# A hand-made order for the first rows, and gaps between the operand places

## The chip, the cores and the metric

The kernel runs on one core of a Trainium2 chip. The metric is the device time of one execution in microseconds; the time before is the median of three runs, 887.15 us (886.62 to 887.22). A profile of one execution shows what each engine did: TensorE (PE, with its weight loads as PEld), VectorE (DVE), ScalarE (ACT), GpSimd (POOL), and SyncE (SP), which here only starts DMAs.

## The reference

From x (2048 tokens by 640 channels, float32) the reference makes the layer-normalized xn, and returns the sum of x, a Fourier mixing of xn and a token MLP on a second normalization of xn:

```
xn = layernorm(x)
a  = xn @ hid_re.T ;  b = xn @ hid_im.T          # 640 x 640 matrices
A  = seq_re @ a - seq_im @ b                     # 2048 x 2048 matrices
h  = layernorm(xn)
u  = gelu(h.T @ w1 + b1)                         # 640 x 1728, over the tokens
B  = (u @ w2 + b2).T
return x + A + B
```

## The kernel before

All products are float32 by three products of halves: an operand is split in a part rounded to the matrix format ("high", made by ACT, line 111) and the rest ("low", made by DVE, line 114), and `three` (lines 119 to 124) issues high by high, high by low and low by high into one PSUM bank. The sums that a fast matrix multiplication (seven products in place of eight) needs are made by DVE between the stages.

The work runs in one list of steps. A step takes one raw piece of a matrix, 128 rows by up to 640 columns, cuts it into high and low in one of three places `cut0` to `cut2`, and issues its products. The piece for step i + 2 is cut while step i multiplies (AHEAD = 2), and raw pieces are loaded some steps earlier by DMAs from SP's queue.

The stages, in order:

- First columns (16 steps, 80 groups of three products): the first eight row blocks of x (128 tokens each), normalized, times the first 512 columns of both 2048-wide matrices. The steps go through the two matrices m = 0 and 1 one after the other, and in each through the eight row blocks k. Each step multiplies by all five 128-channel parts of the row block.
- Seven more column stages of 32 steps, first with the upper half of the rows of x (the operand places `n00` to `n03`), then with the lower half (`n10` to `n13`).
- The hidden matrices, then the MLP up and down. In these the piece is the stationary operand, and the moving one, 320 columns wide, is read from the places that are then called `shid`, `sup` and `sdown`.

In the first columns and the column stages the stationary operand (128 columns) is read from the places `n`, and the moving one (512 columns) from `cut0` to `cut2`. A place `n` is a slab of 17,920 bytes per partition (tags `slab0` to `slab7`: `n00` to `n03` are slab0 to slab3, `n10` to `n13` are slab4 to slab7). The slabs, the pieces (16,384 bytes) and the cuts (5,120 bytes) are all multiples of 256 bytes, so the offset to 256 bytes changes only where small tiles lie between them. Tiles lie in the order in which they are first asked for. `slab7` is asked for first (as `idle`, line 104), at byte 16,672 of the partition: offset 32. Then come three tiles of 128 bytes (`mv`, `norm`, `again`), and then all other places, at offset 160.

| place | offset before | offset after |
| --- | --- | --- |
| n00, n01, n02, n03 | 160, 160, 160, 160 | 0, 64, 96, 128 |
| n10, n11, n12, n13 | 160, 160, 160, 32 | 160, 192, 96, 224 |
| cut0, cut1, cut2 | 160, 160, 160 | 224, 32, 96 |
| raw pieces, results | 160 | 160 |

At the start the rows must be normalized before the first product. The chain for one row block is: DMA of the row block; `moments` (two `bn_stats` and one `bn_aggr` on DVE); `root` (DVE, then a square root on ACT); `inverse` and `offset` (DVE); `normalize` (ACT, in place); `high` (ACT) and `low` (DVE). `first_rows` holds the last three. Twenty products of zeros (WARM, lines 107 and 108) run on TensorE until the data are there. The first eight steps are not recorded under the manual schedule: the scheduling layer orders their instructions on each engine, and from step 8 on they stand as they are written (`by_hand = 8`). ROWS_AT and GROUPS_AT say at which step which rows are loaded and have their factors made.

Of the kernel before, what the change touches and what calls it, by code (L numbers as in the profile page):

```python
# [8 lines left out]
F32 = mybir.dt.float32  # L9
# [5 lines left out]
P = 128  # L15
S = 2048
D = 640
F = 1728
# [10 lines left out]
EPS = 1e-5  # L29
AHEAD = 2  # L30
LOADS = 4
WARM = 20


ROWS_AT = {0: (0,), 1: (1,), 2: (2, 3), 3: (4, 5), 4: (6, 7)}
GROUPS_AT = {0: ((1, 2), (2, 4)), 1: ((4, 6),), 3: ((6, 8),)}

BLOCK = 16
GROUP = 32


# [13 lines left out]
def fnet_plus_mixer(  # L55
# [36 lines left out]

    b1_sb = keep.tile([P, NFB], F32, name="b1_sb")
    b2_sb = keep.tile([P, NS], F32, name="b2_sb")
    out_rows = [out[t * P : (t + 1) * P, :] for t in range(NS)]
    x_rows = [x[t * P : (t + 1) * P, :] for t in range(NS)]
    part_up = [dram.tile([P, 2, D], F32, name=f"up{r}") for r in range(NF2)]
    y_part = [[dram.tile([P, ND, CH], F32, name=f"y{m}{c}") for c in range(NC)] for m in range(2)]


    one = keep.tile([P, 1], F32, name="one")
# [8 lines left out]
    def high(hi, src):  # L110
        nc.scalar.activation(hi, src, AF.Copy)  # L111

    def low(lo, src, hi):
        nc.vector.tensor_sub(lo, src, hi.bitcast(F32))  # L114
# [4 lines left out]
    def three(psum, w, m, first, last):  # L119

        (wh, wl), (mh, ml) = w, m
        nc.tensor.matmul(psum, wh, mh, start=first, stop=False, skip_group_check=True)  # L122
        nc.tensor.matmul(psum, wh, ml, start=False, stop=False, skip_group_check=True)  # L123
        nc.tensor.matmul(psum, wl, mh, start=False, stop=last, skip_group_check=True)  # L124
# [16 lines left out]
    def cut_piece(source, n):  # L141

        held = {}

        def top():
            cut_turn[0] = (cut_turn[0] + 1) % (AHEAD + 1)
            held["piece"] = keep.tile([P, 2, D], R32, name="piece", tag=f"cut{cut_turn[0]}")
            high(held["piece"][:, 0, :n], source())

        def bottom():  # L150
            hi, lo = (held["piece"][:, i, :n] for i in range(2))
            low(lo, source(), hi)
            return hi, lo

        return top, bottom


    mv = keep.tile([P, NS, 2], F32, name="mv")

    norm = keep.tile([P, 2, NS], F32, name="norm")  # L160
    again = keep.tile([P, 2, NS], F32, name="again")
# [29 lines left out]
    def factors(ks):  # L191
        inverse(norm[:, 0, ks], *root(mv[:, ks, 1]))
        offset(norm, ks)
# [15 lines left out]

        return [rooted, inverted]  # L210

    def normalize(k, row, by):
        nc.scalar.activation(row, row, AF.Identity, scale=by[:, 0, k : k + 1], bias=by[:, 1, k : k + 1])  # L213


    def pair_at(tag):
# [27 lines left out]
    def fifth(a, which, i):  # L244
        return a[:, which, 7 * Q + i * P : 7 * Q + (i + 1) * P]

    def place_fixed(h, q):
        fixed[h][q] = keep.tile([P, 2, 8 * Q], R32, name=f"n{h}{q}", tag=f"slab{4 * h + q}")

    def sums_of_rows(h, q, row, lower, apart=False):  # L250
# [37 lines left out]
        return [job1, job2, job3, job4] + [job5] * apart + [job6]  # L288


    x_slab = [
        keep.tile([P, 7, D], F32, name="x0", tag="slab4"), keep.tile([P, 1, D], F32, name="x1", tag="slab5"),
    ]
    x_in = [x_slab[k // 7][:, k % 7, :] for k in range(8)]
# [37 lines left out]
    def later_moments(q):  # L332

        def get():
            for i in range(2):
                nc.sync.dma_start(later_pair(q)[:, i, :], x_rows[8 + q + 4 * i])

        loads[6 + 2 * q].append(get)
        for i in range(2):
            extras[8 + 2 * q + i].append(lambda i=i: moments(8 + q + 4 * i, later_pair(q)[:, i, :]))  # L340

    def later_factors():

# [49 lines left out]
    def c_tile():  # L393

        i = c_turn[0] = (c_turn[0] + 1) % 6
        return c_place[i // 3][:, i % 3, :]

    def store_y(h, m, c, j, t):
        if h == 0:
            nc.gpsimd.dma_start(y_part[m][c][:, j, :], t)  # L400
        else:
            nc.gpsimd.dma_start(y_part[m][c][:, j, :], t, accum_op=ALU.add)

    def first_columns():

        raw = pieces[1].rearrange("p a q c -> p (a q) c")
        banks = {}
        for i in range(BLOCK):
            m, k = i // 8, i % 8

            def load(m=m, k=k, i=i):
                if m == 0:
                    for r in ROWS_AT.get(k, ()):
                        nc.sync.dma_start(x_in[r], x_rows[r])  # L414
                nc.sync.dma_start(raw[:, i % 8, :], dft_seq[m * NC, k])

            def rows(m=m, k=k):
                if m == 0:
                    first_rows(k)
                    for k0, k1 in GROUPS_AT.get(k, ()):  # L420
                        for r in range(k0, k1):
                            moments(r, x_in[r])
                        factors(slice(k0, k1))

            def products(w, m=m, k=k):
                for j in range(ND):
                    if k == 0:
                        banks[j] = psum[(5 * m + j) % 8]
                    three(banks[j], channels(k, j), w, k == 0, k == 7)

            def read(m=m):
                for j in range(ND):
                    c = c_tile()
                    nc.scalar.activation(c, banks[j], AF.Copy)
                    store_y(0, m, 0, j, c)

            loads[i - LOADS].append(load)
            sums[i - AHEAD].append(rows)
            steps.append(cut_piece(lambda i=i: raw[:, i % 8, :], CH) + (products,))
            if k == 7:  # L440
                reads[i + 1].append(read)
        loads[-LOADS].append(lambda: None)

    def columns(g, h, c):

# [363 lines left out]
        )  # L809


    first_columns()
    first_sums = [sums_of_rows(0, q, lambda q=q: x_in[q], lambda q=q: x_in[q + 4], True) for q in range(4)]
    for q in range(4):
        later_moments(q)
    timed[8].append(lambda: jobs.extend(j for part in (slice(4), slice(4, 6)) for js in first_sums for j in js[part]))
    for g in range(2 * NC - 1):
        columns(g, (g + 1) // NC, (g + 1) % NC)
    s_rows = BLOCK
# [37 lines left out]
    for t in range(NS // 2):  # L857
        down(1, t, ("ca", "cb")[t % 2])

    ready = {}  # L860

    def do_jobs(n, short=False):

        while n > 0 and jobs and not (short and isinstance(jobs[0], tuple)):
# [86 lines left out]
```

## Time and profile before

| what | us |
| --- | --- |
| median of three runs | 887.15 |
| the profiled execution | 887.16 |
| its span, first to last instruction | 884.9 |
| PE busy | 877.2 |
| PEld busy | 798.8 |
| DVE busy | 701.8 |
| ACT busy | 525.5 |
| first product of the data (after the products of zeros) | at 9.42 |
| first 320-wide product | at 411.66 |
| last product starts | at 880.78 |

A product's time in the groups (391 ns for 512 columns) is longer than the step from one start to the next, since products overlap in the pipeline. What counts is the step from start to start, which is read from the list of instructions in order of time, or from the number of products in a stretch.

### The profile page before, as it was taken

The page shows a single profiled execution, that of the slowest core. Times are in us where ns is not written, and L with a number is a line of the kernel's source. Part 1 is how long each engine was busy: PE and PEld are TensorE (multiplying, and loading weights), DVE is VectorE, ACT ScalarE, POOL GpSimd, SP SyncE. Part 2 cuts the span into 40 slices and gives each one's busy share as a digit, 9 for nine tenths or more (in the row PEclk, how much of TensorE's full clock was granted, in tenths as well). Part 3 has the DMA queues.
Part 4 walks back from the last instruction along what each step waited for, and adds up shares of the span by engine and source line. Part 5 has one row for each costly group of instructions (what it writes and reads, how often), then busy time and mean ns, then how long its engine had stood idle before and what let it go on. Part 6 is the DMA issues. An engine that isn't in the chain of part 4 may idle for free.

```text
span 884.9 us, 14021 instructions
## 1 busy us (share of the span) xinstructions
PE 877.2 (99%) x4964; PEld 798.8 (90%) x4964; DVE 701.8 (79%) x1181; ACT 525.5 (59%) x953; POOL 123.2 (14%) x166
## 2 busy tenths in 40 slices
PE   8999999999999999999999999999999999999998
PEld 5888888888888888888999999999999999999998
DVE  8577888796787978787877887998678968986776
ACT  6546576664565566557565555675477766655553
POOL 0101000101121111222010101000122211111111
PEclk9999999999999999999999999999999999999999
DMA  8941463719475555869766766553478797756875
GB/s 292 319 144 66 151 253 102 268 48 329 87 206 89 154 136 114 225 83 184 180 124 156 163 142 193 159 180 133 131 170 182 174 253 183 164 129 133 156 173 124
DMA packets 85542, 147.15 MB, mean 166 GB/s; under 512 B 8416, under 2 KB 35296, under 8 KB 85216
## 3 DMA queue, kind: packets, MB, share of 16 engines
q1 hardware_dynamic: 64848, 95.72, 33.3%
q0 software_dynamic: 20624, 50.54, 30.0%
q8 instruction: 39, 0.64, 0.3%
q14 instruction: 31, 0.25, 0.1%
HBM read 99.63 MB, written 51.84 MB: 171 GB/s over the span
## 4 chain that ended last, share of the span: by engine, by line
PE 96%; DVE 2%; ACT 1%; DMA 1%; issue 0%; SPq 0%
PE psum L124 32%; PE psum L123 32%; PE psum L122 32%; DMA pieces<-in_dft_seq 1%; DVE piece L114 0%; DVE st L166 0%; ACT x L213 0%; DVE n L114 0%; DVE shid L114 0%; ACT piece L111 0%; DVE pair L117 0%; DVE pieces L662 0%; DVE pieces L117 0%; SPq L414 0%; ACT shid L111 0%
## 5 line engine op out<-in xcount | busy, mean ns | idle before, releaser
L114 DVE TENSOR_TENSOR piece<-pieces,piece 128x512 fp32r<-128x512 f32 (+2 forms) x506 | 346.6, 688 | 147.7 <-ACT piece L111 144.3
L111 ACT ACTIVATE piece<-pieces 128x512 fp32r<-128x512 f32 (+2 forms) x506 | 317.9, 629 | 235.1 <-PE psum L124 161.0
L122 PE MATMUL psum<-piece,n 128*128 128x512 f32 x584 | 228.4, 391 | 2.5 <-ACT n L111 2.5
L123 PE MATMUL psum<-piece,n 128*128 128x512 f32 x584 | 228.3, 391 | 0.0
L124 PE MATMUL psum<-piece,n 128*128 128x512 f32 x584 | 227.4, 391 | 0.0
L122 PEld LDWEIGHTS psum<-piece,n 128*128 128x128 f32 x584 | 109.6, 188 | 27.2 <-ACT n L111 3.8
L123 PEld LDWEIGHTS psum<-piece,n 128*128 128x128 f32 x584 | 109.7, 188 | 25.6 <-DVE piece L114 2.0
L124 PEld LDWEIGHTS psum<-piece,n 128*128 128x128 f32 x584 | 109.7, 188 | 23.1
L124 PE MATMUL psum<-sup,piece 128*128 128x320 f32 x392 | 121.5, 310 | 0.0
L124 PE MATMUL psum<-sdown,piece 128*128 128x320 f32 x392 | 121.1, 309 | 0.0
L123 PE MATMUL psum<-sdown,piece 128*128 128x320 f32 x392 | 121.0, 309 | 0.0
L123 PE MATMUL psum<-sup,piece 128*128 128x320 f32 x392 | 121.0, 309 | 0.0
L122 PE MATMUL psum<-sup,piece 128*128 128x320 f32 x392 | 121.0, 309 | 0.0
L122 PE MATMUL psum<-sdown,piece 128*128 128x320 f32 x392 | 121.0, 309 | 0.0
L117 DVE TENSOR_TENSOR pieces<-pieces 128x512 f32<-128x512 f32 (+3 forms) x142 | 112.5, 793 | 2.6
L124 PE MATMUL psum<-shid,piece 128*128 128x320 f32 x280 | 86.9, 310 | 0.1
L123 PE MATMUL psum<-shid,piece 128*128 128x320 f32 x280 | 86.5, 309 | 0.0
L122 PE MATMUL psum<-shid,piece 128*128 128x320 f32 x280 | 86.5, 309 | 0.0
L712 ACT ACTIVATE pair<-psum 128x320 f32<-128x320 f32 x104 | 45.3, 436 | 60.1 <-PE psum L124 59.6
L124 PEld LDWEIGHTS psum<-sup,piece 128*128 128x128 f32 x392 | 73.6, 188 | 0.3
L122 PEld LDWEIGHTS psum<-sup,piece 128*128 128x128 f32 x392 | 73.6, 188 | 0.0
L123 PEld LDWEIGHTS psum<-sup,piece 128*128 128x128 f32 x392 | 73.6, 188 | 0.0
(95 smaller groups left out, 1007.8 us busy)
## 6 DMA issues: line engine op xcount, KB each, us to landing
pieces<-in_dft_seq SPq DMA_DIRECT2D x128, 256.0 KB, 5.6
pieces<-in_w SPq DMA_DIRECT2D x88, 256.0 KB, 3.8
y<-c POOLq DMA_DIRECT2D x84, 256.0 KB, 6.0
out<-pair POOLq DMA_DIRECT2D x38, 320.0 KB, 5.2
pieces<-y SPq DMA_DIRECT2D x32, 320.0 KB, 3.7
pieces<-in_w SPq DMA_DIRECT2D x32, 192.0 KB, 3.1
out<-in_x SPq DMA_DIRECT2D x16, 320.0 KB, 5.9
up<-pair POOLq DMA_DIRECT2D x8, 640.0 KB, 3.3
```

Of the source, the lines that this page charges most:

```text
L111: nc.scalar.activation(hi, src, AF.Copy)
L114: nc.vector.tensor_sub(lo, src, hi.bitcast(F32))
L117: nc.vector.tensor_sub(to, a, b)
L122: nc.tensor.matmul(psum, wh, mh, start=first, stop=False, skip_group_check=True)
L123: nc.tensor.matmul(psum, wh, ml, start=False, stop=False, skip_group_check=True)
L124: nc.tensor.matmul(psum, wl, mh, start=False, stop=last, skip_group_check=True)
L712: nc.scalar.activation(c, b, AF.Copy)
```

## The change

The order of the first columns is written out. `FIRST` lists 18 steps as (m, k, first part, last part): row blocks 0 and 1 are multiplied by both matrices at once (all five parts with m = 0, three parts with m = 1), then row blocks 2 to 7 with m = 0, then 2 to 7 with m = 1, and at the end the two parts that were left of blocks 0 and 1 with m = 1. Within a step the products go by kind: high by high for all parts, then high by low, then low by high. `START` is a string of words, one for each operation up to step 7, in the order in which they are recorded, now all under the manual schedule: x and b load, T and B cut, M, R, F make moments, root and factors, H normalizes straight into the high part, N normalizes in place (for later sums), L makes the low part, P multiplies, e loads later rows. Row block 0 comes in two halves, one from ACT's queue ahead of its first work and one from SP's. WARM is 13 in place of 20.

`mv`, `norm` and `again` are asked for ahead of all places, and `pad` puts a tile of 32 or 64 bytes, filled once by POOL, between the places: the offsets are in the table above. The numbers of products, cuts, row operations and stores are the same; there are ten small fills on POOL, one more DMA and one more ACT instruction. The order of the last two jobs of `first_sums` changes, and they start at step 10 in place of 8.

```
-WARM = 20
-ROWS_AT = {0: (0,), 1: (1,), 2: (2, 3), 3: (4, 5), 4: (6, 7)}
-GROUPS_AT = {0: ((1, 2), (2, 4)), 1: ((4, 6),), 3: ((6, 8),)}
-BLOCK = 16
+WARM = 13
+BLOCK = 18
+FIRST = (
+    [(0, 0, 0, 5), (1, 0, 0, 3), (0, 1, 0, 5), (1, 1, 0, 3)] + [(0, k, 0, 5) for k in range(2, 8)]
+    + [(1, k, 0, 5) for k in range(2, 8)] + [(1, 0, 3, 5), (1, 1, 3, 5)]
+)
+START = """
+    x0 b0 x1 b1 b2 x2 b3 x3 b4 x4 x5 b5 x6 x7 b6 b7
+    T0 M0 R0 F0 H0 B0 N0 M1 R1 T1 L0 F1 H1 B1 P0
+    M2 T2 N1 B2 L1 b8 P1 M3 T3 R2-3 F2-3 H2 B3 P2
+    M4 T4 N2 B4 L2 b9 P3 M5 H3 T5 R4-5 N3 B5 F4-5 L3 b10 e0 P4
+    M6 H4 T6 N4 B6 L4 b11 P5 H5 M7 R6-7 T7 N5 B7 F6-7 L5 b12 e1 P6
+    H6 T8 M8 N6 B8 L6 b13 P7 H7 T9 M12 N7 B9 L7
+"""
+    def pad(n):
+        gap = keep.tile([P, n // 4], F32, name=f"gap{gaps[0]}")
+        gaps[0] += 1
+        nc.gpsimd.memset(gap, 0.0)
+    x_slab = [keep.tile([P, 7, D], F32, name="x0", tag="slab4")]
+    pad(32)
+    x_slab.append(keep.tile([P, 1, D], F32, name="x1", tag="slab5"))
+    pad(32)
+    nc.scalar.dma_start(x_in[0][:, H2:], x_rows[0][:, H2:])
...
         def top():
+            if gaps[0] < 10:
+                pad(64)
...
     for q in range(4):
+        pad((32, 64, 32, 32)[q])
         place_fixed(0, q)
+    pad(32)
-    def first_rows(k):
-        normalize(k, x_in[k], norm)
+    def first_rows(k, which):
...
-        high(two(0), src)
-        high(fifth(a, 0, k // 4), x_in[k][:, 2 * Q :])
-        low(two(1), src, two(0))
-        low(fifth(a, 1, k // 4), x_in[k][:, 2 * Q :], fifth(a, 0, k // 4))
+        for to, t in whole:
+            if which == 0:
+                normalize(k, t, norm, to(0))
+            else:
+                low(to(1), t, to(0))
...
+            for n, (rows, cols) in enumerate(((0, 0), (0, 1), (1, 0))):
+                for j in range(j0, j1):
...
+                    nc.tensor.matmul(
+                        banks[m, j], channels(k, j)[rows], w[cols], start=n == 0 and k == begin,
+                        stop=n == 2 and k == end, skip_group_check=True,
+                    )
...
-    by_hand = 8
-    for i in range(-LOADS, by_hand):
-        if i == -AHEAD:
-            moments(0, x_in[0])
-            factors(slice(0, 1))
-        turn_of(i, 0)
     with tc.manual_schedule():
-        for i in range(by_hand, len(steps) + 1):
+        for word in START.split():
+            start[word[0]](*map(int, word[1:].split("-")))
+        for i in range(8, len(steps) + 1):
```

More of the change, by code (lines that the diff above doesn't have):

```diff
@@ L31 @@
 LOADS = 4
-WARM = 20
-ROWS_AT = {0: (0,), 1: (1,), 2: (2, 3), 3: (4, 5), 4: (6, 7)}
-GROUPS_AT = {0: ((1, 2), (2, 4)), 1: ((4, 6),), 3: ((6, 8),)}
-BLOCK = 16
+WARM = 13
[4 more added lines that the diff above has]
+)
+FIRST_AT = [0, 6, 1, 7, 2, 3, 4, 5, 0, 1, 2, 3, 4, 5, 0, 1, 6, 7]
+START = """
[6 more added lines that the diff above has]
+"""
 GROUP = 32
@@ L94, in fnet_plus_mixer @@
     b2_sb = keep.tile([P, NS], F32, name="b2_sb")
+    one = keep.tile([P, 1], F32, name="one")
+    mv = keep.tile([P, NS, 2], F32, name="mv")
+    norm = keep.tile([P, 2, NS], F32, name="norm")
+    again = keep.tile([P, 2, NS], F32, name="again")
+    def pad(n):
+        gap = keep.tile([P, n // 4], F32, name=f"gap{gaps[0]}")
+        gaps[0] += 1
+        nc.gpsimd.memset(gap, 0.0)
+    gaps = [0]
     out_rows = [out[t * P : (t + 1) * P, :] for t in range(NS)]
     x_rows = [x[t * P : (t + 1) * P, :] for t in range(NS)]
+    x_slab = [keep.tile([P, 7, D], F32, name="x0", tag="slab4")]
+    pad(32)
+    x_slab.append(keep.tile([P, 1, D], F32, name="x1", tag="slab5"))
+    pad(32)
+    x_in = [x_slab[k // 7][:, k % 7, :] for k in range(8)]
+    nc.scalar.dma_start(x_in[0][:, H2:], x_rows[0][:, H2:])
     part_up = [dram.tile([P, 2, D], F32, name=f"up{r}") for r in range(NF2)]
     y_part = [[dram.tile([P, ND, CH], F32, name=f"y{m}{c}") for c in range(NC)] for m in range(2)]
-    one = keep.tile([P, 1], F32, name="one")
     nc.vector.memset(one, 1.0)
@@ L155, in cut_piece @@
         return top, bottom
-    mv = keep.tile([P, NS, 2], F32, name="mv")
-    norm = keep.tile([P, 2, NS], F32, name="norm")
-    again = keep.tile([P, 2, NS], F32, name="again")
     def moments(k, row):
@@ L210, in factors_again, with normalize @@
         return [rooted, inverted]
-    def normalize(k, row, by):
-        nc.scalar.activation(row, row, AF.Identity, scale=by[:, 0, k : k + 1], bias=by[:, 1, k : k + 1])
+    def normalize(k, row, by, to=None):
+        nc.scalar.activation(
+            row if to is None else to, row, AF.Identity, scale=by[:, 0, k : k + 1], bias=by[:, 1, k : k + 1]
+        )
     def pair_at(tag):
@@ L288, in sums_of_rows @@
         return [job1, job2, job3, job4] + [job5] * apart + [job6]
[L291 to L294, printed above, removed]
     for q in range(4):
+        pad((32, 64, 32, 32)[q])
         place_fixed(0, q)
-    def first_rows(k):
-        normalize(k, x_in[k], norm)
+    pad(32)
+    def first_rows(k, which):
         a = fixed[0][k % 4]
@@ L307, in two @@
             return part(a, which, 1, 2).rearrange("p (b c) -> p b c", b=2)
-        high(two(0), src)
-        high(fifth(a, 0, k // 4), x_in[k][:, 2 * Q :])
-        low(two(1), src, two(0))
-        low(fifth(a, 1, k // 4), x_in[k][:, 2 * Q :], fifth(a, 0, k // 4))
+        whole = [(two, src), (lambda which: fifth(a, which, k // 4), x_in[k][:, 2 * Q :])]
+        if which == 0 and k == 0:
+            whole[:1] = [(lambda which, b=b: two(which)[:, b, :], src[:, b, :]) for b in range(2)]
+        for to, t in whole:
[3 more added lines that the diff above has]
+                low(to(1), t, to(0))
     def channels(k, j):
@@ L330, in later_pair, with later_load, later_moments @@
         return later[0][:, q] if q < 3 else later[1]
[L332 to L338, printed above, removed]
+    def later_load(q):
         for i in range(2):
-            extras[8 + 2 * q + i].append(lambda i=i: moments(8 + q + 4 * i, later_pair(q)[:, i, :]))
+            nc.sync.dma_start(later_pair(q)[:, i, :], x_rows[8 + q + 4 * i])
+    def later_moments(k):
+        moments(k, later_pair(k % 4)[:, (k - 8) // 4, :])
     def later_factors():
@@ L407, in first_columns @@
         banks = {}
[L408 to L441, printed above, removed]
@@ L442, in first_columns, with load, products @@
-        loads[-LOADS].append(lambda: None)
+        vq = {}
+        def load(i):
+            m, k = FIRST[i][:2]
+            nc.sync.dma_start(raw[:, FIRST_AT[i], :], dft_seq[m * NC, k])
+        def products(w, m, k, j0, j1):
+            for n, (rows, cols) in enumerate(((0, 0), (0, 1), (1, 0))):
+                for j in range(j0, j1):
+                    begin, end = (2, 1) if m == 1 and j >= 3 else (0, 7)
+                    if n == 0 and k == begin:
+                        banks[m, j] = psum[(5 * m + j) % 8]
+                    nc.tensor.matmul(
+                        banks[m, j], channels(k, j)[rows], w[cols], start=n == 0 and k == begin,
+                        stop=n == 2 and k == end, skip_group_check=True,
+                    )
@@ new lines, in read @@
+        def read(m, js):
+            for j in js:
+                c = c_tile()
+                nc.scalar.activation(c, banks[m, j], AF.Copy)
+                store_y(0, m, 0, j, c)
+        for i, (m, k, j0, j1) in enumerate(FIRST):
+            steps.append(
+                cut_piece(lambda i=i: raw[:, FIRST_AT[i], :], CH)
+                + (lambda w, at=(m, k, j0, j1): products(w, *at),)
+            )
+        reads[10].append(lambda: read(0, range(ND)))
+        reads[16].append(lambda: read(1, range(3)))
@@ new lines, in first_columns, with row, top, bottom @@
+        reads[18].append(lambda: read(1, range(3, ND)))
+        for i in range(14, 16):
+            loads[i - 6].append(lambda i=i: load(i))
+        def row(k):
+            if k == 0:
+                nc.sync.dma_start(x_in[0][:, :H2], x_rows[0][:, :H2])
+            else:
+                nc.sync.dma_start(x_in[k], x_rows[k])
+        def top(i):
+            steps[i][0]()
+        def bottom(i):
+            ready[i] = steps[i][1]()
+        def run(i):
+            steps[i][2](ready.pop(i))
@@ new lines, in rooted, with factored @@
+        def rooted(k, to=None):
+            ks = slice(k, (to or k) + 1)
+            vq[k] = root(mv[:, ks, 1])
+        def factored(k, to=None):
+            ks = slice(k, (to or k) + 1)
+            inverse(norm[:, 0, ks], *vq[k])
+            offset(norm, ks)
+        return {
+            "x": row, "b": load, "e": later_load, "T": top, "B": bottom, "P": run,
+            "M": lambda k: moments(k, x_in[k]) if k < 8 else later_moments(k), "R": rooted, "F": factored,
+            "H": lambda k: first_rows(k, 0), "N": lambda k: normalize(k, x_in[k], norm),
+            "L": lambda k: first_rows(k, 1),
+        }
@@ L809, in down @@
         )
-    first_columns()
+    ready = {}
+    start = first_columns()
     first_sums = [sums_of_rows(0, q, lambda q=q: x_in[q], lambda q=q: x_in[q + 4], True) for q in range(4)]
-    for q in range(4):
-        later_moments(q)
-    timed[8].append(lambda: jobs.extend(j for part in (slice(4), slice(4, 6)) for js in first_sums for j in js[part]))
+    for q in range(2, 4):
+        loads[4 + 2 * q].append(lambda q=q: later_load(q))
+    for i, k in enumerate((9, 13, 10, 14, 11, 15)):
+        extras[8 + i].append(lambda k=k: later_moments(k))
+    timed[10].append(lambda: jobs.extend(
+        [j for js in first_sums for j in js[:4]] + [j for q in (2, 3, 0, 1) for j in first_sums[q][4:]]
+    ))
     for g in range(2 * NC - 1):
@@ L858, in fnet_plus_mixer @@
         down(1, t, ("ca", "cb")[t % 2])
-    ready = {}
     def do_jobs(n, short=False):
```

## The prediction

> **What bounds the kernel now.** I read the page's busy shares first, then the chain that ended last, then stretches of the run with the number of products in each, and last the list of instructions in order of time, at the start and around one operand place.
>
> ```profile
> PE 877.2 (99%) x4964; PEld 798.8 (90%) x4964; DVE 701.8 (79%) x1181; ACT 525.5 (59%) x953; POOL 123.2 (14%) x166
> ...
> PE 96%; DVE 2%; ACT 1%; DMA 1%; issue 0%; SPq 0%
> ...
> PE psum L122 <- ACT n L111: 2.5, 3, 1.5
> ...
> 20.00:213.60 193.60, 193.60 (x851) 158.80 (x849) 150.01 (x269) 115.83 (x213) 20.61 (x38) 1.00 0.50 176
> 213.60:402.00 188.40, 188.40 (x824) 154.38 (x823) 147.67 (x212) 108.65 (x183) 32.93 (x39) 1.00 0.62 147
> ...
> 589.00:735.00 146.00, 146.00 (x997) 146.00 (x996) 117.58 (x193) 97.20 (x184) 25.35 (x32) 1.00 0.68 175
> ```
>
> TensorE is the bound: 96% of the chain, at full clock (1.00) in every stretch. So a change can act in two ways only: it takes away time in which TensorE has no product, or it changes the step from one product to the next. Idle time is small after the start; the third line is the only wait for operands of real products, 2.5 us over three times, all before 18 us.
>
> The step differs by stage. With 320 columns it is 146.0/995 = 0.1467 us. With 512 columns the undisturbed step is 0.2267 (317.62 to 318.30 below is three of them). The stretch from 213.6 holds some 822 products, which would take 186.3 at that step, and takes 188.4. The 2.1 us too many lie in one place:
>
> ```profile
> 317.62 0.39 PE L123 MATMUL psum<-piece,n 128*128 128x512 f32 x1
> 317.84 0.39 PE L124 MATMUL psum<-piece,n 128*128 128x512 f32 x1
> 318.07 0.39 PE L122 MATMUL psum<-piece,n 128*128 128x512 f32 x1
> 318.30 0.39 PE L123 MATMUL psum<-piece,n 128*128 128x512 f32 x1
> 318.52 0.40 PE L124 MATMUL psum<-piece,n 128*128 128x512 f32 x1
> 318.76 0.40 PE L122 MATMUL psum<-piece,n 128*128 128x512 f32 x1
> 319.00 0.40 PE L123 MATMUL psum<-piece,n 128*128 128x512 f32 x1
> ...
> 320.38 0.40 PE L123 MATMUL psum<-piece,n 128*128 128x512 f32 x1
> 320.62 0.40 PE L124 MATMUL psum<-piece,n 128*128 128x512 f32 x1
> 320.86 0.40 PE L122 MATMUL psum<-piece,n 128*128 128x512 f32 x1
> ```
>
> By the program's order the nine products from 318.76 take their weights from n13, those before from n12. The nine on n13 take 320.86 - 318.76 = 2.10 us, 0.233 each; the nine before them 2.05, of which the last, under which n13's first weights load, has 0.24. So it goes each time n13 comes, and the first five to nine products on n10 after it are uneven too (0.224 to 0.236). n13 is the one place whose offset to 256 bytes (32) is not that of all others (160).
>
> The start, by ACT and TensorE:
>
> ```profile
> 5.47 1.91 PEld L108 LDWEIGHTS <-idle 128*128 128x128 bf16 x9 [0.28 <-issue]
> ...
> 7.19 0.63 ACT L111 ACTIVATE piece<-pieces 128x512 fp32r<-128x512 f32 x1 [1.82 <-DMA pieces<-in_dft_seq]
> 7.73 0.91 ACT L213 ACTIVATE x<-x,norm 128x640 f32<-128x640 f32 x1
> ...
> 8.75 0.81 ACT L111 ACTIVATE n<-x 128x512 fp32r<-128x512 f32 x2
> ...
> 9.42 0.50 PE L122 MATMUL psum<-piece,n 128*128 128x512 f32 x1 [1.54 <-ACT n L111]
> ```
>
> The factors of row block 0 are ready at 7.25, but ACT first waits for the second matrix piece (7.19), cuts it, normalizes 640 columns in place and only then makes the high part. Steps 0 to 2 are 45 products, 45 x 0.2267 = 10.20 us; step 3 starts at 21.34. So the stage runs as if it had started at 11.14 without a wait.
>
> **The change, part by part.**
>
> *First product.* x lands at 3.82 and its scaled variance is there at 5.13, square root 5.17 to 5.37, as before. Then four small DVE operations; in a later chain of this kind they start 0.2 apart (19.47, 19.66, 19.85, 20.05), and nothing of row 1 and no cut (0.69) stands between them now: 5.43 + 0.8 = 6.23. ACT makes 256 columns of the high part straight from x in 0.41 (mean of ten such), so the first product can start at about 6.75; the thirteen products of zeros end near 6.3. The other columns follow at 7.1 and 7.4, and are needed at 7.2 and 7.66. High by low is due at 7.9 and its cut ends at 6.92. Low by high is due at 9.03; DVE has by then the moments of row 1 (1.15 + 0.15) and the low part (0.69), to 8.94. That is a narrow margin.
>
> *The following rows.* DVE needs for a row 1.15 (moments), 0.69 (cut), 0.97 (low) and half of a pair's factors, some 0.5: 3.3 us, where a step of 15 products lasts 3.40. The first four steps are 48 products (10.9 us) for two rows, which is the slack that the added matrix gives. Followed word by word with these rows, I find one wait of 0.3, at step 3 (cut of its piece behind the factors of rows 2 and 3). So the stage runs as from 7.1: 11.14 - 7.1 = 4.0 saved. Bounds: 1.5 if each of steps 2 to 7 waits 0.4 more for DVE, 4.6 if the two halves of x land 0.3 sooner and nothing waits.
>
> *Queues.* On SP the pieces b1 and b3 pass ahead of rows 2 and 3 (0.45 per issue); x2 is the sixth issue, at about 3.3, and its moments are not due before 10. ACT's DMA issue (0.43 on SP) stands before its table load (1.28), done by 2.6, and its first work comes at 4.43. The ten fills take 0.1 each on POOL, whose first store is due after 36. The split of row 0 costs ACT one instruction, counted above. All these: 0.
>
> *End of the stage.* Steps 16 and 17 have six products, 1.36 us, against 0.69 for the cut and some 0.8 for a job on DVE; the cuts run two steps ahead. Parts 3 and 4 of m = 1 use banks 0 and 1 again 0.68 after step 10 begins, where ACT needs 0.6 to empty each; bank 0 is done four products before. 0, at most 0.4. The fewer zeros and the reordered jobs lie off TensorE's path: 0.
>
> *The gaps.* n13 leaves offset 32. I take its price (2.1) as gone: no weights of the 512-wide stages stand at 32 any more. Other offsets than 32 and 160 have no row. Bounds for a 512-wide product: 0.224, the lowest step after n13, to 0.233, n13's own; over 1752 products that is -4.7 to +11.0 against 0.2267. I take 0.2267, since six of the eight places are as near to 160 as to 32 or nearer (n00 and n01 are not). For 320 columns cut1 puts a third of the weights at 32, and the moving operands vary. There the only row is a moving operand at 32 (slab7 again): 0.44 us for three products (560.02 to 560.46), as for the three after it. The nine products after a wait there take 1.31 (412.51 to 413.82), 0.1456 each, so uneven steps need not cost. Take 0; bounds: -0.0011 on 3192 products, -3.5, and n13's price (0.0064) on the third at 32, +6.8.
>
> **Sum.** Made against the profiled execution, 887.16 (0.01 above the median; 2.2 us lie around its span): 887.16 - 4.0 - 2.1 = 881.1.
>
> **Rivals.**
>
> *A: each change of offset costs, not offset 32.* n13 is dear because weights and moving operand, or one place and the next, differ. For it: n10 is at 160 and is uneven for its first five to nine products after n13, and a step has six to nine products, so with a new offset in each step it would never settle. Against: the moving operand at 32 costs nothing with 320 columns. Then 1752 products go at 0.2325 or so: +10.2, less the 2.1 already paid, less 4.0 for the start: 891.3. It decides from 6.1 us, that is from 3.5 ns per 512-wide product over 0.2267.
>
> *B: the gaps shorten the step everywhere.* The step is 13.3 ns above what columns alone explain in both widths (0.2267 and 0.1467 differ by 80 ns for 192 columns, 0.4167 ns each, so 512 take 0.2133). The zeros show less: nine loads in 1.91 us, (1.91 - 0.15)/8 = 0.220 as shown, with one place for all. If steps fell to the lowest seen, 0.224 and 0.144: -4.7 - 8.5, with the start 870 (n13's 2.1 on top: 868). Against: bf16 is another type, and the low steps are always followed by high ones.
> The Trainium skill (TensorE: Matmul & The Clock Gate, "Wait — 56ns, not 53.3ns?") gives a warm step of columns/2.4 GHz + 2.5 ns, an estimate of 0.2157 for 512; the trace agrees for the zeros only and not for float32, 0.2267.
>
> *C: offsets have no say,* and n13's price belongs to its turn in the step. Then only the start counts: 883.1. Against: n03, the same turn with the upper rows, has the plain step (849 products in 193.6 us are 192.4 plus known waits).
> The Trainium skill says it so (same page, "Step-by-step: what each phase is for"): TensorE has two read ports, and loading the next weights takes nothing from the running product's reads. By that rule the sum is 883.1; the 0.233 of n13 speaks against it.
>
> *D: the start saves little,* because DVE falls behind: 1.5 saved, n13's price back, something lost to uneven steps: about 886.
>
> **Numbers.** Changes below 0.2% (1.8 us) count as same. Chances: forecast 0.42, A 0.28, B 0.13, C 0.11, D 0.06. Faster (below 885.4): forecast, B and C but a little, 0.63; same 0.08 (D and the mild end of A); slower (above 888.9) 0.29. The range for 8 in 10 leaves out the far ends of A and B: 869 to 892. The forecast's own range is 879 to 884, from the bounds of the start.
>
> **What would show it.** After: first product near 6.75, few waits to 20 us; in the column stages n13 like its neighbours, 0.2267 per product; 0.1467 in the 320-wide stages. It is wrong if the 512-wide stretches hold fewer products per us than 4.41 throughout (A), if the 320-wide ones hold more than 6.82 (B), or if TensorE waits for DVE between 8 and 30 us (D).

## The result, and the profile after

The changed kernel takes 889.59 us (median of 8 runs, 889.26 to 890.53); the kernel before, run beside it, 887.17 (8 runs, 886.62 to 887.49). The ratio is 1.0029, with a 95% interval of 1.0019 to 1.0040: slower by 0.3%, where a gain of 0.7% was forecast. The profiled execution of the changed kernel took 889.51, of which 887.6 are its span.

The page of the changed kernel: the busy time of TensorE, and the engines' shares of the chain that ended last.

```profile
PE 882.5 (99%) x4957; PEld 799.3 (90%) x4957; DVE 706.6 (80%) x1183; ACT 529.4 (60%) x956; POOL 123.8 (14%) x176
...
PE 98%; DVE 1%; ACT 0%; DMA 0%; issue 0%; SPq 0%
```

The two last steps of the first columns cut the pieces of row blocks 0 and 1 a second time, so a piece is cut 508 times here and 506 times before, on ACT and on DVE (the text ahead of the prediction calls the numbers of cuts the same); TensorE has no wait at these steps.

TensorE has 98% of the chain in place of 96%. It waits less, and yet the kernel ends later. So the steps from one product to the next must have become longer. The same stretches as before (stretch; then busy time and number of instructions of PE, PEld, DVE, ACT, POOL; granted clock; DMA share; GB/s):

```profile
20.00:213.60 193.60, 193.60 (x833) 155.85 (x832) 155.36 (x289) 119.00 (x218) 20.63 (x38) 1.00 0.52 181
213.60:402.00 188.40, 188.40 (x814) 152.60 (x813) 145.85 (x210) 107.25 (x181) 32.97 (x39) 1.00 0.62 147
589.00:735.00 146.00, 146.00 (x994) 145.88 (x993) 117.92 (x193) 97.13 (x183) 23.88 (x31) 1.00 0.68 177
```

The two 512-wide stretches hold 833 and 814 products, where they held 851 and 824. The clock is 1.00 as before, so it is not the clock. The 320-wide stretch has 994 in place of 997.

The start went nearly as forecast (list of instructions, in order of time):

```profile
4.94 0.20 ACT L205 ACTIVATE q<-v 128x1 f32<-128x1 f32 x1
...
5.83 0.16 DVE L220 SCALAR_TENSOR_TENSOR norm<-mv,norm 128x1 f32<-128x1 f32 x1
...
6.02 1.48 ACT L244 ACTIVATE n<-x,norm 128x256 fp32r<-128x256 f32 x3 [0.88 <-DVE norm L220]
...
6.68 0.74 PE L453 MATMUL psum<-piece,n 128*128 128x512 f32 x2 [0.31 <-ACT n L244]
```

The first product starts at 6.68 (before: 9.42), and after it the table of waits names only one more wait for operands, of 0.2 us.

For a balance I went through the starts of all products in both traces. The plain step is 0.2267 us for 512 columns and 0.1467 for 320. A start more than 45 ns later than that counts as a wait, whatever caused it (so these sums are larger than the table's); whatever else is above or below the plain step counts as unevenness.

| us | before | after | difference |
| --- | --- | --- | --- |
| first product starts at | 9.42 | 6.68 | -2.74 |
| waits after it | 3.57 | 1.49 | -2.08 |
| unevenness of the 1752 products of 512 columns | 2.64 | 9.73 | +7.09 |
| unevenness of the 3192 products of 320 columns | 0.02 | 0.87 | +0.85 |
| last product starts at | 880.78 | 883.92 | +3.13 |

Behind the last product the changed kernel is 0.5 shorter (its span is only 2.6 longer, 887.6 against 884.9), and 0.3 less lies around its span; that makes the 2.4 by which the times differ. The start saved what it should. The 512-wide products took back more than that.

Where? Three steps of a column stage, taken by their places, show it. Each step reads its moving operand from one cut, and the three cuts take turns from step to step. From 64.91 to 67.01 nine products read weights from n01 (offset 64) and the cut at 32; then nine read n02 (96) and the cut at 96; then nine read n03 (128) and the cut at 224. (In the order in which the steps first ask for them the cuts stand at 224, 32 and 96. The program starts its turn with cut1, so these are cut1, cut2 and cut0; the table ahead of the prediction has these offsets one number off.)

```profile
64.91 0.39 PE L156 MATMUL psum<-piece,n 128*128 128x512 f32 x1
...
66.77 0.40 PE L158 MATMUL psum<-piece,n 128*128 128x512 f32 x1
67.01 0.39 PE L156 MATMUL psum<-piece,n 128*128 128x512 f32 x1
67.24 0.39 PE L157 MATMUL psum<-piece,n 128*128 128x512 f32 x1
67.47 0.39 PE L158 MATMUL psum<-piece,n 128*128 128x512 f32 x1
67.69 0.39 PE L156 MATMUL psum<-piece,n 128*128 128x512 f32 x1
...
69.06 0.40 PE L156 MATMUL psum<-piece,n 128*128 128x512 f32 x1
...
71.17 0.40 PE L156 MATMUL psum<-piece,n 128*128 128x512 f32 x1
```

The nine in the middle take 69.06 - 67.01 = 2.05 us, the plain step; those on either side take 2.10 and 2.11, 0.233 and 0.234 each, as dear as n13 was before. The cheap ones are those whose weights and moving operand have the same offset. The same order of places and cuts gives every product of the seven column stages its pair. Without the first three products and the last of each step, the step is 228.8 ns on average where the offsets are equal, 229.1 where they differ by 64 (moving minus weights, modulo 256), and 231.9 to 234.4 at the other six differences. That is the theory that the experiments had to test: **the difference between the two offsets costs, not any one offset, and not a change from place to place.** Its rivals: offset 32 is bad in itself; every change of offset from one place to the next costs; or the new order of the first columns costs something in the steps behind it.

### The profile page after: what moved, and what is told of

It is laid out like the page before. It is cut to its first block, busy times and chain, and to the rows that moved or that the text cites. A ratio compares the mean times of both kernels' runs of the same rounds, so it can differ in the third digit from the quotient of the medians.

```text
span 887.6 us, 14021 instructions
## 1 busy us (share of the span) xinstructions
PE 882.5 (99%) x4957; PEld 799.3 (90%) x4957; DVE 706.6 (80%) x1183; ACT 529.4 (60%) x956; POOL 123.8 (14%) x176
## 4 chain that ended last, share of the span: by engine, by line
PE 98%; DVE 1%; ACT 0%; DMA 0%; issue 0%; SPq 0%
PE psum L158 31%; PE psum L157 30%; PE psum L156 30%; PE psum L453 6%; DMA pieces<-in_dft_seq 0%; DVE piece L148 0%; DVE shid L148 0%; ACT piece L145 0%; DVE pair L151 0%; DVE pieces L724 0%; ACT shid L145 0%; DVE pieces L151 0%; ACT pair L676 0%; ACT n L244 0%; ACT c L573 0%
## 5 line engine op out<-in xcount | busy, mean ns | idle before, releaser
L158 PE MATMUL psum<-piece,n 128*128 128x512 f32 x504 | 198.8, 394 | 0.0
L157 PE MATMUL psum<-piece,n 128*128 128x512 f32 x504 | 198.8, 394 | 0.0
L156 PE MATMUL psum<-piece,n 128*128 128x512 f32 x504 | 198.7, 394 | 0.0
L157 PEld LDWEIGHTS psum<-piece,n 128*128 128x128 f32 x504 | 94.7, 188 | 23.1 <-DVE piece L148 0.8
L156 PEld LDWEIGHTS psum<-piece,n 128*128 128x128 f32 x504 | 94.7, 188 | 22.2
L158 PEld LDWEIGHTS psum<-piece,n 128*128 128x128 f32 x504 | 94.7, 188 | 22.2
L158 PEld LDWEIGHTS psum<-sup,piece 128*128 128x128 f32 x392 | 73.8, 188 | 0.2
L158 PEld LDWEIGHTS psum<-sdown,piece 128*128 128x128 f32 x392 | 73.7, 188 | 0.0
L157 PEld LDWEIGHTS psum<-sup,piece 128*128 128x128 f32 x392 | 73.6, 188 | 0.0
```

## The experiments

The first four kernels ran together, and so did the last four. The kernel before had a median of 886.28 in the first group and of 886.74 in the second (13 runs each); ratios are against those.

### e1: the new order without gaps

```
     def pad(n):
+        if n == 0:
+            return
...
-    pad(32)
+    pad(0)
...
+    cut_gaps = [0, 0, 0, 0]
...
-            if gaps[0] < 10:
-                pad(64)
+            if cut_gaps:
+                pad(cut_gaps.pop(0))
...
-        pad((32, 64, 32, 32)[q])
+        pad((0, 0, 0, 0)[q])
```

(`cut_gaps` holds the gaps ahead of the first cut, ahead of the others, and behind the third.) All places and cuts then stand at 160, n13 too, since `mv`, `norm` and `again` are still asked for first.

> The changed kernel without its gaps: order of the first rows as changed, all places and cuts at offset 160. The profile of after has products on weights and moving operand of the same offset (n02 and cut2, both 96) at 0.2267 per product and nearly all others near 0.2325. Theory 'equal offsets' (the step is short where weights and moving operand have the same offset to 256 bytes): all 512-wide products at 0.2267, 1752 x 0.0056 = 9 us below after and n13's toll gone too: 881. Theory 'offset 32 is bad, the rest of the loss is the new order': about 887, the 512-wide stretches still hold fewer products than 4.41 per us.

Measured: 881.78 us (880.97 to 883.15, 4 runs), ratio 0.9943 (0.9926 to 0.9960). The same stretches of this kernel:

```profile
20.00:213.60 193.60, 193.60 (x851) 158.78 (x850) 157.18 (x294) 121.78 (x223) 21.63 (x40) 1.00 0.53 189
213.60:402.00 188.40, 188.40 (x832) 155.59 (x831) 150.18 (x215) 111.34 (x188) 33.56 (x39) 1.00 0.62 147
589.00:735.00 146.00, 146.00 (x998) 146.00 (x997) 117.40 (x192) 97.03 (x185) 25.33 (x32) 1.00 0.69 178
```

851 and 832 products, where the changed kernel had 833 and 814: 18 fewer in each stretch of about 190 us. So the gaps cost the time, and the new order costs the later steps nothing. At the last product the two traces are 7.7 apart: 9.15 of unevenness at 512 columns and 0.85 at 320, less 0.74 by which this run's first product came later (its first matrix piece came later, below at e6), less 1.54 of waits that the changed kernel does not have.

### e2: the gaps without the new order

The kernel before, with `mv`, `norm`, `again` and x asked for first and with gaps that give each place the offset it has after:

```
+    x_slab = [keep.tile([P, 7, D], F32, name="x0", tag="slab4")]
+    pad(32)
+    x_slab.append(keep.tile([P, 1, D], F32, name="x1", tag="slab5"))
+    pad(32)
...
+            if gaps[0] < 10:
+                pad(64)
...
     for q in range(4):
+        pad((32, 64, 32, 32)[q])
         place_fixed(0, q)
+    pad(32)
```

> The kernel before with the gaps alone: places and cuts at the offsets of the changed kernel, first rows in the old order. If the two parts of the change add, the gaps cost what after loses against the kernel without gaps, 7 to 9 us less the 2.1 that n13 cost: 893 to 894, and 4 us more than after. If the loss came from the new order (DVE behind), it is at 887 or below.

Measured: 893.82 us (893.34 to 894.65, 4 runs), ratio 1.0083 (1.0068 to 1.0098).

```profile
20.00:213.60 193.60, 193.60 (x832) 155.78 (x831) 147.59 (x265) 113.25 (x208) 19.56 (x36) 1.00 0.47 167
213.60:402.00 188.40, 188.40 (x813) 152.43 (x812) 145.15 (x210) 108.49 (x182) 34.02 (x41) 1.00 0.61 152
```

832 and 813 products, as in the changed kernel (833 and 814). The gaps alone cost 7.5 us, and bring the slow step with them into the old order. Its column stage begins at 66.77, that of the changed kernel at 62.82: the new order is worth 3.95 with the same gaps in both.

### m1: products alone, eight offsets by eight

Eight places of weights and eight of moving operands at the offsets 0, 32, ... 224, and every pair 36 times with 512 columns and 24 times with 320. It was profiled once, and all its operands are zeros.

```
+    with tc.manual_schedule():
+        run(ws[7], ms[7], CH, 12)
+        for w in ws:
+            for m in ms:
+                run(w, m, CH, 12)
+        for w in ws:
+            for m in ms:
+                run(w, m, H2, 8)
```

> Only products, on zeros: eight weight places and eight moving tiles at the offsets 0 to 224 in steps of 32, each with each, 36 products of 512 columns and then 24 of 320 columns per pair; x is copied to the output and all else is left out. Theory 'equal offsets': eight of the 64 pairs (equal ones) at 0.2267, the others 0.230 to 0.236 for 512 columns; about 0.1467 for all with 320. Theory 'changes of offset': every pair settles at 0.2267 after the first nine products. A pair below 0.2267 would be a better layout than any so far.

The list of instructions for the weights `wb` at offset 160, with moving operands `ma` to `mf` at 128, 160, 192, 224, 0 and 32 (start; duration of the group; 36 products each):

```profile
117.53 8.55 PE L110 MATMUL psum<-ma,wb 128*128 128x512 f32 x36
125.92 8.35 PE L110 MATMUL psum<-mb,wb 128*128 128x512 f32 x36
134.11 8.57 PE L110 MATMUL psum<-mc,wb 128*128 128x512 f32 x36
142.51 8.41 PE L110 MATMUL psum<-md,wb 128*128 128x512 f32 x36
150.76 8.57 PE L110 MATMUL psum<-me,wb 128*128 128x512 f32 x36
159.17 8.56 PE L110 MATMUL psum<-mf,wb 128*128 128x512 f32 x36
```

From start to start: 8.39, then 8.19 for the pair with equal offsets, 8.40, 8.25, 8.41. The first products of each 36 are uneven; the second half of each group, averaged over all pairs with the same difference (moving minus weights, modulo 256), gives:

| difference | 0 | 32 | 64 | 96 | 128 | 160 | 192 | 224 |
| --- | --- | --- | --- | --- | --- | --- | --- | --- |
| ns a product, 512 columns | 226.7 | 233.4 | 228.8 | 233.5 | 233.4 | 234.3 | 233.3 | 233.2 |

For all eight offsets of the weights the row is the same within about 1 ns, so in this run the difference alone counts. n13 before, at 32 with the cuts at 160, has a difference of 128: 233.4 here, 0.233 us there. With 320 columns all 64 pairs lie between 146.2 and 146.8. The table needs no fitting to give the kernel: averaged over the pairs that occur in the changed kernel, it is 232.95 for n00 to n03 with the three cuts and 231.6 for n10 to n13 (which have two pairs with equal offsets and two at +64 among twelve). The trace of the changed kernel has 232.8 and 231.8 in these stages.

### e3: one difference for all, 64 bytes

e1 with 64 bytes ahead of the first cut, and 192 behind the third: all places n at 160, all cuts at 224. No place changes its offset against the one before it; only the difference between weights and moving operand is left.

```
-    cut_gaps = [0, 0, 0, 0]
+    cut_gaps = [64, 0, 0, 192]
```

> The changed kernel with all weights' places at 160 and all three cuts at 224: no offset changes from step to step, but weights and moving operand always differ by 64. Theory 'equal offsets': 512-wide products near 0.2325 throughout, 881 + 10 = 891. Theory 'each change of offset unsettles the next five to nine products': nothing changes, so 0.2267 and 881. For 320 columns (weights in the cuts, moving operand in the places) both expect 0.1467 within 0.0005.

Measured: 887.97 us (885.03 to 889.02, 10 runs), ratio 1.0014 (1.0004 to 1.0024): 6.2 above e1.

```profile
20.00:213.60 193.60, 193.60 (x843) 157.59 (x842) 156.42 (x292) 121.01 (x221) 21.51 (x40) 1.00 0.53 186
213.60:402.00 188.40, 188.40 (x809) 152.62 (x808) 145.88 (x209) 106.22 (x178) 32.01 (x38) 1.00 0.60 143
```

A difference without any change costs, so the rival that each change costs does not explain it. But the size is not what m1 gives. With the upper rows (first stretch) the step averages 229.6, near m1's 228.8; with the lower rows (second stretch) 233.3, at the same difference of 64. Both go on evenly for hundreds of products. So at this difference the step can settle at two values, and the ten runs, which spread over 4.0 us, would fit a choice that is not always made alike. What chooses was not found.

### e4: all at 32

e1 with a single gap of 128 bytes ahead of everything: places and cuts all at 32.

```
-    pad(0)
+    pad(128)
     x_slab = [keep.tile([P, 7, D], F32, name="x0", tag="slab4")]
```

> The changed kernel with every place, cut and raw piece at offset 32 (one gap of 128 ahead of all). Theory 'equal offsets': as without gaps, the ratio to before 0.994 and the 512-wide step 0.2267. The forecast's theory 'offset 32 is bad for weights': n13's step of 0.233 for all eight places, 1752 x 0.0064 = 11 us more, ratio above 1.006.

Measured: 881.15 us (880.41 to 881.41, 4 runs), ratio 0.9935 (0.9920 to 0.9950).

```profile
213.60:402.00 188.40, 188.40 (x832) 155.49 (x831) 150.09 (x216) 111.69 (x188) 33.64 (x39) 1.00 0.63 147
```

832 products, as many as with everything at 160. Offset 32 is not bad.

### e5: n13 put right in the kernel before

The kernel before, with one edit: `mv`, `norm` and `again` are asked for ahead of `idle`, so that slab7 and with it n13 stand at 160.

```
+    mv = keep.tile([P, NS, 2], F32, name="mv")
+    norm = keep.tile([P, 2, NS], F32, name="norm")
+    again = keep.tile([P, 2, NS], F32, name="again")
     idle = keep.tile([P, CH], BF16, name="idle", tag="slab7")
...
-    mv = keep.tile([P, NS, 2], F32, name="mv")
-    norm = keep.tile([P, 2, NS], F32, name="norm")
-    again = keep.tile([P, 2, NS], F32, name="again")
```

> The kernel before with one edit: the three small tiles are asked for ahead of slab7, so that n13 too stands at 160. First rows in the old order. Both theories: n13's 2.1 us go, about 884, and the stretch from 213 to 402 holds the plain step of 0.2267 throughout. If n13 was dear for its turn in the step, nothing changes.

Measured: 884.81 us (884.09 to 886.35, 10 runs), ratio 0.9980 (0.9970 to 0.9989): 1.9 gained. In the list of instructions 36 products in a row, which is once through all four places, now go evenly:

```profile
313.67 0.39 PE L128 MATMUL psum<-piece,n 128*128 128x512 f32 x1
...
317.52 0.39 PE L127 MATMUL psum<-piece,n 128*128 128x512 f32 x1
...
319.56 0.39 PE L127 MATMUL psum<-piece,n 128*128 128x512 f32 x1
...
321.83 0.39 PE L128 MATMUL psum<-piece,n 128*128 128x512 f32 x1
```

321.83 - 313.67 = 8.16, or 0.2267 each. The nine on n13, from 317.52 to 319.56, take 2.04 where they took 2.10 before; n13 no longer stands out. So its price did not come from its turn in the step. The unevenness of all 512-wide products falls from 2.64 to 0.69.

### e6: the root ahead of the first cut

In e1's profiled run the first product came at 7.42 and not at 6.68. There the first matrix piece landed late, and ACT had been told to cut it before it takes the square root (list of instructions of e1, ACT):

```profile
5.17 0.63 ACT L148 ACTIVATE piece<-pieces 128x512 fp32r<-128x512 f32 x1 [2.49 <-DMA pieces<-in_dft_seq]
5.71 0.19 ACT L211 ACTIVATE q<-v 128x1 f32<-128x1 f32 x1
```

In the changed kernel the same cut began at 4.37 and the root at 4.94. The edit, on e1, puts the cut behind the root:

```
-    T0 M0 R0 F0 H0 B0 N0 M1 R1 T1 L0 F1 H1 B1 P0
+    M0 R0 T0 F0 H0 B0 N0 M1 R1 T1 L0 F1 H1 B1 P0
```

> The changed kernel without gaps, and the square root of row block 0 ahead of the first cut on ACT (M0 R0 T0 in place of T0 M0 R0). In the run without gaps the first matrix piece landed at 5.17 and held up the square root till 5.71, though its input was there at 4.68, and the first product came at 7.42; in the run with gaps the piece came at 4.37 and the first product at 6.68. Expected: first product between 6.7 and 6.9 whenever the piece lands by 5.3, and 0 to 0.7 us less than without this edit: 881.0 to 881.8. A rival: the cut then ends later than the high part and the first product waits for it, no gain.

Measured: 881.35 us (881.20 to 881.67, 4 runs), ratio 0.9939 (0.9924 to 0.9954). The list of instructions of this kernel, ACT:

```profile
4.93 0.20 ACT L211 ACTIVATE q<-v 128x1 f32<-128x1 f32 x1 [2.25 <-DVE v L210]
5.04 0.61 ACT L148 ACTIVATE piece<-pieces 128x512 fp32r<-128x512 f32 x1
6.01 1.48 ACT L250 ACTIVATE n<-x,norm 128x256 fp32r<-128x256 f32 x3 [0.36 <-DVE norm L226]
```

The root comes at 4.93 though the cut starts only at 5.04; the first product is at 6.66, and the four runs lie within 0.5 us where e1's lay within 2.2. Against e4 (881.15, beside it) it shows no gain in the median: e4 keeps the order of root and cut as it was, and its first product came at 6.91. e1, e4 and e6 are all faster than both kernels, by 4.5 to 5.6 us than the one before, which ran beside them.

### m2: finer differences, other widths, alternation

The same kind of kernel, again profiled once and on zeros, with moving operands at fifteen differences to one place of weights, three differences at eight widths, and blocks of nine products in alternation.

```
+        for m in ms:
+            run(wa, m, CH, 12)
+        for n in (256, 320, 384, 416, 448, 480, 496, 512):
+            for m in ns:
+                run(wa, m, n, 12)
+        for _ in range(4):
+            run(wa, ns[0], CH, 3)
+            run(wb, ns[2], CH, 3)
+        for _ in range(4):
+            run(wa, ns[0], CH, 3)
+            run(wb, ns[0], CH, 3)
```

> Only products on zeros again (x is copied to the output, all else is left out). First one weight place and moving tiles 0 to 252 bytes further in fine steps, 36 products of 512 columns each: expected 0.2267 at 0, 0.2288 at 64 and 0.232 to 0.2345 elsewhere; whether a few bytes already cost is open. Then 256 to 512 columns at differences 0, 64 and 128: the two widths seen so far say no cost at 320 and 6 ns at 512; a cost in proportion to columns would give 2 ns at 416, a threshold none or all. Last, blocks of nine products that change offset: weights and moving operand both 0, then both 128, and so on, against a fixed moving operand with weights 0 and 128 in turn. If only equality counts, the first holds 0.2267 but for a few products after each change; if each change costs, both are near 0.232.

The list of instructions: `ma` has difference 0, `mb` 4 bytes, `mc` 8, `mo` -4; `na` and `nc` have 0 and 128 to the weights `wa`, and `nc` has 0 to `wb`, `na` -128.

```profile
39.03 8.32 PE L112 MATMUL psum<-ma,wa 128*128 128x512 f32 x36
47.19 8.68 PE L112 MATMUL psum<-mb,wa 128*128 128x512 f32 x36
55.70 8.55 PE L112 MATMUL psum<-mc,wa 128*128 128x512 f32 x36
...
155.93 8.34 PE L112 MATMUL psum<-mo,wa 128*128 128x512 f32 x36
164.11 4.47 PE L112 MATMUL psum<-na,wa 128*128 128x256 f32 x36
...
326.56 2.21 PE L112 MATMUL psum<-na,wa 128*128 128x512 f32 x9
328.61 2.21 PE L112 MATMUL psum<-nc,wb 128*128 128x512 f32 x9
330.66 2.21 PE L112 MATMUL psum<-na,wa 128*128 128x512 f32 x9
...
345.01 2.27 PE L112 MATMUL psum<-na,wb 128*128 128x512 f32 x9
347.12 2.25 PE L112 MATMUL psum<-na,wa 128*128 128x512 f32 x9
349.21 2.25 PE L112 MATMUL psum<-na,wb 128*128 128x512 f32 x9
351.30 2.21 PE L112 MATMUL psum<-na,wa 128*128 128x512 f32 x9
```

*Alternation.* From 326.56 on both offsets jump by 128 together every nine products: 2.05 us a block, as without any change. From 345.01 only the weights jump: 2.11 for a block with unequal offsets, 2.09 for the equal one that follows it, then 2.09 and 2.05. So a change alone costs nothing that lasts; what it costs is the inequality, and a few products after it that are still uneven.

*Fine differences.* From start to start, the 36 products take 8.16 at 0, 8.51 at 4 bytes and 8.18 at -4. Settled steps in ns: 0: 226.65; 4 bytes: 236.65; 8: 233.2; 16: 231.9; 32: 233.2; 64: 228.8; 128: 232.9; 208: 234.5; 240 (-16): 226.7; 248 (-8): 229.9; 252 (-4): 226.65. It is not symmetric: four bytes ahead cost 10 ns, four bytes behind nothing.

*Widths.* What a step has above 0.4167 ns a column, in ns, for differences 0 / 64 / 128: 256 columns 13.3 / 11.1 / 11.75; 320: 13.4 / 13.4 / 13.2; 384: 13.35 / 13.3 / 16.2; 448: 16.0 / 13.3 / 16.8; 512: 13.3 / 15.55 / 18.7. At 256 unequal offsets are even the faster ones, by 2 ns; from 384 up they can cost, and 448 is fastest at 64. No rule that I know from these numbers gives all of them.

## Why the prediction was wrong

*First product* (about 6.75): 6.68. The path was right, and the nearness of the number is partly luck. The factors were ready at 5.99 and not at 6.23, nearly all of it because x landed sooner (its moments start at 3.59, not 3.82), and the first 256 columns of the high part took 0.60 and not 0.41.

*The following rows* (4.0 saved; a narrow margin on DVE): right. Two starts come 0.1 late where the margin was called narrow (8.9 to 9.6), and in place of the wait of 0.3 at step 3 there is one of 0.07. The column stage begins at 62.82 where it began at 65.54, 2.7 earlier; in the first 240 products the first product gives 2.74, fewer waits 1.21 (0.39 in place of 1.60), and unevenness, which belongs to the gaps, takes back 1.23 (1.35 in place of 0.12). Without that it is 3.95. Rival D is out. Without gaps, the order is worth 884.81 - 881.35 = 3.5 (e5 to e6) or 3.7 (e5 to e4) in the medians.

*Queues* and *End of the stage* (0, at most 0.4): nothing in the waits contradicts it; in the table of waits TensorE waits 0.3 for ACT at its first product and 0.2 once for a cut, near 80 us.

*The gaps*: here it failed, in the sentences "I take its price (2.1) as gone: no weights of the 512-wide stages stand at 32 any more" and "I take 0.2267, since six of the eight places are as near to 160 as to 32 or nearer". The price is rightly sized: 1.9 in e5. But I read it as a property of offset 32, and it is one of the difference between n13 (32) and the cuts (160). e4, with everything at 32, has the plain step. Offset 32 was gone, but 21 of the 24 pairs of place and cut now differ, and the 1752 products have 9.73 us of unevenness in place of 2.64, 5.6 ns each. The bounds (0.224 to 0.233) held the 0.2322 that was measured; the value taken inside them was at the wrong end.

Two rows that I showed pointed the other way. The first five to nine products on n10 after n13 were uneven, at an offset that was like all others. And n13 differed from its partners in a second respect, its distance to the cuts, which the rows could not separate from its offset; "nearer to 160" chose between the two without evidence. The moving operand at 32, which I took against rival A, was a 320-wide row, and m1 shows that at this width no pair of offsets costs anything (146.2 to 146.8).

For 320 columns I took 0; it was +0.85 in the changed kernel, inside the bounds. It comes with the gaps: e2 has 0.92 of it, and the kernel before and the kernels with equal offsets (e1, e4, e5, e6) have 0.02 or less. But e3, with one unequal difference throughout, has 0.01, and no pair of m1 shows it. Offsets that change every few products at this width were not tried alone, so its cause is open.

*Rival A* came nearest, with 891.3 against 889.6. Its reason named two things at once, and the runs part them: "weights and moving operand differ" is right (m1, e3), "each change of offset costs" is not (m2's first alternation; e3 has the dear step without a change from place to place). It gave +4.1 where the traces have +3.13 at the last product: 1.0 less unevenness and 0.8 more saved at the start and in waits, against 0.85 more at 320 columns. *Rival B* is out, with 833 and 814 products where it needed more than 851 and 824. *Rival C* had offsets without a say, and n13's price as one of its turn: e5 refutes it. The rule of the Trainium skill that stands beside it (TensorE: Matmul & The Clock Gate, "Step-by-step: what each phase is for": the load of the next weights takes nothing from the running product's reads) does not hold as a rule of time in these runs: 226.7 ns with equal offsets, 233.4 at a difference of 128, with nothing else changed. Whether it is the reads of the two operands that meet was only argued, since no run here changes one without the other.

Had the gaps been left out, both terms of the sum would have stood nearly as forecast: 3.5 to 3.7 for the order and 1.9 for n13 in the medians, against 4.0 and 2.1. The times of e4, e6 and e1 (881.15 to 881.78, against 881.1) look closer than that by luck: the kernel before was 0.4 to 0.9 faster beside them than in the profiled execution that the sum starts from, so they gain 4.5 to 5.6 on it, and not 6.1.

## What to carry to other kernels

When one row of a trace is dear and differs from its neighbours in one number, ask whether it is the number or its distance to a partner's, and price both before you choose. With float32 products of 512 columns, each with its own weights, keep stationary and moving places a whole number of 256 bytes apart, by asking for small tiles first, and look again whenever a small tile is added: here that is worth 1.9 us for one place in eight (e5), and 7.7 where most differ (e1). Read such a cost from start to start by operand place, since the mean duration (394 ns against 391) and the busy share (99% both times) hardly move.

## What the runs showed that I had not expected

- In m1 the step of a 512-wide product depends on the difference of the two offsets modulo 256 and on neither offset itself: eight offsets of the weights give the same row, from 226.7 to 234.3 ns. In m2, 4 bytes ahead give 236.65 where 4 bytes behind give 226.65.
- It depends on the width without a simple order: nothing at 320 columns, up to 3 ns at 384, 5 to 8 for most differences at 512, and a small gain at 256.
- At a difference of 64 the step settles at about 229 ns in some stages and at 233.3 in others, and the time of the whole kernel spreads over 4.0 us (885.03 to 889.02), where kernels with equal offsets spread over 0.5 to 2.3. Why was not settled.
- Where the gaps slow TensorE, it waits a little less: the changed kernel has 1.5 us of waits fewer than e1 and 1.0 fewer than e6. That the cuts had more time is likely, but no run tried it.
